# Half of the first V tile loaded by GpSimd's queue instead of SyncE's, at the start of a fused attention and feed-forward kernel

## The chip, the cores and the metric

The kernel runs on one core of a Trainium2 chip. The metric is the device time of one execution in microseconds (us), the median of three runs. Engine names: PE is TensorE (matmuls), PEld its weight load, DVE is VectorE, ACT is ScalarE, POOL is GpSimd, SP is SyncE. "SPq" and "POOLq" are the DMA issues on the queues of SP and POOL.

## What is computed

```python
# q, k, v: 8 batches x 8 heads x 576 tokens x 64, float32
q_c, k_c, v_c = (a.reshape(B, H, nc, 64, D) for a in (q, k, v))      # chunks of 64 tokens
scores = np.matmul(q_c, k_c.transpose(0, 1, 2, 4, 3)) / np.sqrt(D)
attn = exp(scores - max) ; attn = attn / (sum(attn) + 1e-09)
x = np.matmul(attn, v_c)  ->  reshaped to 4608 tokens x 512
h = np.maximum(x @ w_in, 0.0)          # w_in 512 x 2048
out = h * h @ w_out                    # w_out 2048 x 512, result float32
```

Attention never looks across a chunk of 64 tokens, so a block of tokens can go through attention and both matrix products on its own.

## The kernel before

The 4608 tokens are cut into nine blocks of 512 tokens. For each block the kernel computes attention into `xT` (x transposed, bfloat16), then `ffn_in` (x times w_in, 64 matmuls of 128x512 for a block, ReLU on ACT, square on DVE or ACT) and `ffn_out` (times w_out). From the second block on, attention for the next block is woven into the matmuls of the block before it by a table of slots. The order on every engine is the order in which the program calls the operations; no scheduler changes it.

The first block has nothing to hide behind, so it has its own path (lines 656 to 697), in two halves of four heads each, u = 0 and u = 1:

- `load_half` (L227) loads q and k of four heads and 512 tokens with one DMA of 512 KB each, on SP's queue. The calls go q of u=0, k of u=0, q of u=1, k of u=1.
- `load_v_half(u)` (L236) loads V of four heads and 512 tokens into `v_first` with four DMAs of 128 KB, one for each 128 tokens (t = 0 to 3), in rows of 64 float32 (256 bytes). `v_first` is a view of the buffer `w_sum`, which has its real use only later; the profile therefore calls it w_sum. A POOL memset (L220) puts a column of ones beside each head of V.
- `load_w_in(i)` (L162 and the casts at L165) loads 256 columns of w_in (512 KB) on SP's queue into a staging tile `w_st`, of which there are five, and POOL casts it to bfloat16. The first of the eight casts is cut into two pieces, one for each 128 columns. `load_w_out(i)` (L170, cast at L173) does the same for w_out.
- On PE the order is: transposes of q and k of u=0 (L257), scores (L278), transposes of q and k of u=1, `values_half(e0, ..., 0, 0)` (L298: attention weights of u=0 times V, tokens t = 0 and 1), scores of u=1, `values_half(e0, ..., 0, 1)`, transposes of x (L314), `values_half(e1, ..., 1, 0)`, and so on to the last transposes of x at L314. Matmuls on constants (`keep_busy`, L326) stand in between. After them come the 64 matmuls of `ffn_in` (L480). The first two output tiles of `ffn_in` begin with the two quarters of the sum that need only heads 0 to 3.

The DMAs on SP's queue take eight completion counters in turn, so the n-th load carries a wait for the (n-8)-th to have landed. DMAs issued from POOL have counters of their own.

Of the kernel before, what the change touches and what calls it, by code (L numbers as in the profile page):

```python
# [17 lines left out]
def kernel(  # L18
# [9 lines left out]
    nc = tc.nc  # L28
# [130 lines left out]
    def load_w_in(i, n_cast=1):  # L159
        cols = slice(i * 256, (i + 1) * 256)  # L160
        st = wst_pool.tile([128, 1024], FP32, name="w_st").rearrange("p (a f) -> p a f", a=n_dt)
        nc.sync.dma_start(out=st, in_=moe_w_in[:, cols].rearrange("(a p) f -> p a f", p=128))  # L162
        n = 256 // n_cast
        for c in range(0, 256, n):
            nc.gpsimd.tensor_copy(  # L165
                out=w_in_bf[:, :, i * 256 + c:i * 256 + c + n], in_=st[:, :, c:c + n])
# [57 lines left out]
    def load_half(src, u, name):  # L224
        st = in_pool.tile([128, 2, H, D], FP32, name=name)
        b, s = first
        nc.sync.dma_start(  # L227
            out=st.rearrange("p t h d -> p (t h d)").rearrange("p (h e) -> p h e", h=4),
            in_=src[b, 4 * u:4 * u + 4, s:s + BT, :].rearrange("h (s i) d -> s h (i d)", i=4))
        return st.bitcast(BF16).rearrange("p t h d -> p (t h d)").rearrange(  # L230
            "p (h i d) -> p h i d", h=4, i=4)

    def load_v_half(u):
        b, s = first
        for t in range(4):
            nc.sync.dma_start(  # L236
                out=v_first[:, t, 4 * u:4 * u + 4, 0:D],
                in_=v[b, 4 * u:4 * u + 4, s + 128 * t:s + 128 * t + 128, :].rearrange(
                    "h s d -> s h d"))
# [419 lines left out]
    for u in range(2):  # L659
        qh.append(load_half(q, u, "q_sb"))  # L660
        kh.append(load_half(k, u, "k_sb"))
    for u in range(2):
        load_v_half(u)
    load_w_in(0, n_cast=2)
    xTs[0] = att_pool.tile([128, BT // 128, n_dt, 128], BF16, name="xT", bufs=2)
    qkTs = [att_pool.tile([128, 2, 2, n_hp, 128], BF16, name="qkT", bufs=4) for _ in range(2)]
# [146 lines left out]
```

## Time and profile before

| what | value |
|---|---|
| median of 3 runs | 281.04 us (280.75 to 281.83) |
| the profiled execution | 281.17 us, of which its span is 279.4 us |
| PE busy | 269.2 us, 96% of the span |
| DVE, ACT, POOL busy | 186.5, 160.5, 35.8 us |
| DMA moved | 57.09 MB, mean 204 GB/s |
| q1 (the queue that SP issues to) | 83.8% of 16 DMA engines' span |
| q0 (the queue that POOL issues to) | 2.8% of 16 DMA engines' span |
| first matmul of `ffn_in` (L480) | starts 17.63 us into the span |

The span is the time from the first to the last event that the profile shows; 1.8 us of the execution lie outside of it. In answers of the trace, each line names the start, the duration, the engine, the line of the kernel, the operation, its output and input, the number of instructions merged, and in brackets how long the engine was idle before it and what ended that idle time. In the answers by stretch of time, DMA share is the mean busy share of the 16 DMA engines (it can pass 1.00, as packets overlap within an engine).

### The profile page before, as it was taken

How to read it: one execution, taken by the hardware profiler on the slowest of the kernel's cores; microseconds unless marked ns; L12 is line 12 of the kernel's file. 1: busy time of each engine (PE TensorE's matmuls, PEld its weight loads, DVE VectorE, ACT ScalarE, POOL GpSimd, SP SyncE). 2: the span in 40 equal slices, each digit the busy share in tenths (PEclk: the TensorE clock that was granted, in tenths of full speed). 3: DMA queues.
4: the chain of work that ended last, by engine and by line, in shares of the span. 5: the costliest groups of instructions: out<-in, count | busy, mean ns of one | idle time of the engine just before them, and what ended most of it. 6: DMA issues, size and time to landing. Idle time of an engine off the chain costs nothing.

```text
span 279.4 us, 7179 instructions
## 1 busy us (share of the span) xinstructions
PE 269.2 (96%) x2960; PEld 176.2 (63%) x2963; DVE 186.5 (67%) x304; ACT 160.5 (57%) x269; POOL 35.8 (13%) x62
## 2 busy tenths in 40 slices
PE   6789999989999999999999999999999999999994
PEld 4544455878774487448744874487448744874584
DVE  1446414998943595579549954995579649955793
ACT  2537615885348862877197719762877197218710
POOL 2037844240171000000000000000000000000012
PEclk9999999999999999999999999999999999999998
DMA  7999999989999999979999999979699964141003
GB/s 236 220 345 358 364 332 240 326 212 194 255 207 244 238 213 191 258 183 198 218 245 260 187 184 298 191 158 185 196 238 208 212 199 40 39 109 44 0 21 131
DMA packets 144384, 57.09 MB, mean 204 GB/s; under 512 B 110624, under 2 KB 141600, under 8 KB 144352
## 3 DMA queue, kind: packets, MB, share of 16 engines
q1 hardware_dynamic: 143296, 53.62, 83.8%
q0 software_dynamic: 912, 2.88, 2.8%
q8 instruction: 23, 0.38, 0.6%
q10 hardware_dynamic: 144, 0.13, 0.1%
q14 instruction: 9, 0.07, 0.1%
HBM read 36.70 MB, written 9.44 MB: 165 GB/s over the span
## 4 chain that ended last, share of the span: by engine, by line
PE 80%; DVE 6%; SPq 4%; ACT 2%; DMA 2%; issue 2%; POOL 0%; DVEq 0%; ACTq 0%
PE ps_ffn L480 39%; PE ps_ffn L533 32%; PE ps_ffn L626 5%; SPq L236 3%; DMA w_st<-in_moe_w_in_dram 2%; DVE x L409 2%; DVE gT L475 2%; DVE w_st L493 2%; ACT rl L471 2%; PE ps_att L401 2%; PE ps_att L374 1%; ACT e L385 1%; SPq L227 1%; PE ps_att L428 1%; PE ps_att L190 1%
## 5 line engine op out<-in xcount | busy, mean ns | idle before, releaser
L480 PE MATMUL ps_ffn<-xT,w_in_bf 128*128 128x512 bf16 (+1 forms) x640 | 130.0, 358 | 0.7 <-POOL w_in_bf L165 0.7
L475 DVE TENSOR_TENSOR gT<-rl 128x512 bf16<-128x512 f32 (+2 forms) x132 | 74.2, 593 | 61.4 <-ACT rl L471 60.7
L471 ACT ACTIVATE rl<-ps_ffn 128x512 f32<-128x512 f32 (+2 forms) x160 | 85.7, 554 | 26.9 <-PE ps_ffn L480 23.3
L480 PEld LDWEIGHTS <-w_in_bf 128*128 128x128 bf16 x640 | 60.5, 98 | 58.2 <-POOL w_in_bf L165 2.2
L533 PEld LDWEIGHTS <-w_st 128*128 128x128 bf16 x640 | 62.0, 98 | 8.2 <-DVE w_st L493 0.9
L493 DVE TENSOR_TENSOR w_st<-gT 128x2048 bf16<-128x2048 bf16 x40 | 47.3, 1217 | 0.2
L533 PE MATMUL ps_ffn<-w_out_bf,w_st 128*128 128x256 bf16 x384 | 45.1, 273 | 0.1
L533 PE MATMUL ps_ffn<-w_sum,w_st 128*128 128x256 bf16 x256 | 29.6, 273 | 0.0
L616 ACT COPY o_sb<-ps_ffn 128x512 f32<-128x512 f32 (+1 forms) x8 | 4.5, 559 | 40.3 <-PE ps_ffn L533 40.3
L533 PEld LDWEIGHTS <-gT 128*128 128x128 bf16 x256 | 24.8, 98 | 4.4 <-DVE gT L475 0.2
L568 POOL DMA_DIRECT2D out_dram<-o_sb x4 | 2.2, 553 | 186.2 <-DVE o_sb L493 186.2
L409 DVE TENSOR_TENSOR x<-ps_att,rec 128x512 bf16<-128x512 f32 x32 | 22.1, 691 | 1.1
L385 ACT ACTIVATE e<-ps_att 128x1024 bf16<-128x1024 f32 x16 | 15.8, 1022 | 4.8 <-PE ps_att L374 4.8
L473 ACT ACTIVATE gT<-rl 128x512 bf16<-128x512 f32 (+2 forms) x28 | 16.8, 599 | 0.9
L533 PE MATMUL ps_ffn<-w_out_bf,gT 128*128 128x256 bf16 x128 | 15.3, 273 | 0.0
L533 PE MATMUL ps_ffn<-w_sum,gT 128*128 128x256 bf16 x128 | 15.3, 273 | 0.0
L626 PE MATMUL ps_ffn<-w_out_bf,gT 128*128 128x512 bf16 x61 | 14.2, 379 | 0.3 <-issue 0.2
L165 POOL CAST w_in_bf<-w_st 128x1024 bf16<-128x1024 f32 (+1 forms) x9 | 9.0, 1001 | 17.9 <-DMA w_st<-in_moe_w_in_dram 17.9
L340 ACT CAST qkb<-k_sb 128x1024 bf16<-128x1024 f32 x10 | 10.5, 1047 | 1.2 <-DMA k_sb<-in_k_dram 1.2
L333 ACT CAST qkb<-q_sb 128x1024 bf16<-128x1024 f32 x10 | 10.4, 1044 | 0.0
L626 PEld LDWEIGHTS <-gT 128*128 128x128 bf16 x64 | 6.0, 98 | 7.0
L401 PEld LDWEIGHTS <-e 64*64 64x64 bf16 x512 | 5.8, 107 | 6.3 <-DVE x L409 2.1
(63 smaller groups left out, 157.1 us busy)
## 6 DMA issues: line engine op xcount, KB each, us to landing
q_sb<-in_q_dram SPq DMA_DIRECT2D x16, 512.0 KB, 6.2
k_sb<-in_k_dram SPq DMA_DIRECT2D x24, 256.0 KB, 5.8
out_dram<-o_sb SPq DMA_DIRECT2D x20, 256.0 KB, 3.7
w_st<-in_moe_w_in_dram SPq DMA_DIRECT2D x8, 512.0 KB, 6.8
w_st<-in_moe_w_out_dram SPq DMA_DIRECT2D x8, 512.0 KB, 6.1
ve_sb<-in_v_dram SPq DMA_DIRECT2D x28, 128.0 KB, 3.5
vo_sb<-in_v_dram SPq DMA_DIRECT2D x21, 128.0 KB, 3.0
out_dram<-o_sb POOLq DMA_DIRECT2D x9, 256.0 KB, 5.5
```

Source lines behind the costliest of these rows:

```text
L333: copy(out=qkb[:, 0].rearrange("p (i h d) -> p i h d", i=2, h=H), in_=qk[g][0].rearrange("p t h d -> p (t h d)").rearrange("p (h i d) -> p ...
L340: copy(out=state["qkb", g][:, 1], in_=qk[g][1].rearrange("p t h d -> p (t h d)"))
L385: nc.scalar.activation(out=e_out, in_=s_in, func=AF.Exp, scale=scale)
L401: nc.tensor.matmul(out=ps[64 * p:64 * p + 64, a, hp * (D + 1):(hp + 1) * (D + 1)], lhsT=e[64 * c:64 * c + 64, a, hp, t, :], rhs=vb[64 * c: ...
L409: nc.vector.tensor_tensor(out=x[:, t].rearrange("p h a d -> p a h d"), in0=o[:, :, :, 0:D], in1=rec.to_broadcast([128, 2, n_hp, D]), op=AL ...
L471: nc.scalar.activation(out=rl[:, 0:n], in_=h[:, 0:n], func=AF.Relu)
L473: nc.scalar.activation(out=gT[:, ft, c:c + n], in_=rl[:, 0:n], func=AF.Square)
L475: nc.vector.tensor_tensor(out=gT[:, ft, c:c + n], in0=rl[:, 0:n], in1=rl[:, 0:n], op=ALU.mult)
L480: nc.tensor.matmul(out=h[:, 0:n], lhsT=w_in_bf[:, dt, ft * 128:(ft + 1) * 128], rhs=xT[:, c // 128:(c + n) // 128, dt, :], start=(dt == 0) ...
L493: engine.tensor_tensor(out=out, in0=in0, in1=in1, op=op)
L533: nc.tensor.matmul(out=outs[t], lhsT=a[:, i, t * 128:(t + 1) * 128], rhs=b[:, i, :], start=(first and i == 0 and (last or t == 0)), stop=( ...
L626: nc.tensor.matmul(out=o_ps[tt], lhsT=gT[:, ft, tt * 128:(tt + 1) * 128], rhs=w_out_bf[:, ft, :], start=(ft == 0), stop=(ft == n_ft - 1))
```

## The change

V of u=1 (heads 4 to 7) is no longer issued by SP behind the q and k of both halves, but by POOL. In the program its call moves up, to stand after q and k of u=0; on POOL it comes behind the memsets and ahead of the casts of w_in. SP issues q, k, q, k, then the four DMAs of V of u=0, then w_in. In the built program the orders on PE, DVE and ACT are the same as before; SP has four DMAs fewer and POOL four more.

```diff
     def load_v_half(u):
         b, s = first
+        queue = nc.gpsimd if u else nc.sync
         for t in range(4):
-            nc.sync.dma_start(
+            queue.dma_start(
                 out=v_first[:, t, 4 * u:4 * u + 4, 0:D],
...
     for u in range(2):
         qh.append(load_half(q, u, "q_sb"))
         kh.append(load_half(k, u, "k_sb"))
-    for u in range(2):
-        load_v_half(u)
+        if u == 0:
+            load_v_half(1)
+    load_v_half(0)
     load_w_in(0, n_cast=2)
```

## The prediction

> **What bounds the kernel now.** I began with the page. PE is busy for 96% of the span, and the chain of work that ended last is PE for most of its length. What is not PE lies partly at the start: the chain by line names SP's issue of V (L236) and a landing of w_in.
>
> ```profile
> PE 80%; DVE 6%; SPq 4%; ACT 2%; DMA 2%; issue 2%; POOL 0%; DVEq 0%; ACTq 0%
> PE ps_ffn L480 39%; PE ps_ffn L533 32%; PE ps_ffn L626 5%; SPq L236 3%; DMA w_st<-in_moe_w_in_dram 2%; DVE x L409 2%; DVE gT L475 2%; DVE w_st L493 2%; ACT rl L471 2%; PE ps_att L401 2%; PE ps_att L374 1%; ACT e L385 1%; SPq L227 1%; PE ps_att L428 1%; PE ps_att L190 1%
> ```
>
> Second, the chain in order of time for the first 24 us. It runs through SP's eight issues of V, then through the third piece of w_in, its cast, and into PE. After that it holds no load: whatever PE gains or loses before 32 us should reach the end one for one.
>
> ```profile
> 11.86 0.51 SPq L236
> ...
> 13.51 6.92 DMA w_st<-in_moe_w_in_dram
> 20.43 0.05 issue
> 20.49 1.23 POOL w_in_bf L165
> 21.71 0.05 issue
> 21.76 2.33 PE ps_ffn L480 x10
> ```
>
> Third, the timeline of the first 45 us, to see how far behind the other path, attention, is.
>
> ```profile
> 2.11 0.15 POOL L220 MEMSET w_sum<- 128x32 f32 x1
> 2.89 9.48 SPq L236 DMA_DIRECT2D w_sum<-in_v_dram  x8
> 9.85 0.64 PE L257 MATMUL ps_ffn<-ident,k_sb 128*64 128x128 bf16 x16 [0.66 <-DMA k_sb<-in_k_dram]
> 11.03 0.32 PE L298 MATMUL ps_att<-w_sum,e 64*64 64x65 bf16 x8 [0.17 <-DMA w_sum<-in_v_dram]
> 12.41 9.69 SPq L162 DMA_DIRECT2D w_st<-in_moe_w_in_dram  x8
> 16.86 0.40 PE L314 MATMUL ps_ffn<-ident,x 128*128 128x128 bf16 x4 [0.59 <-DVE x L306]
> 17.63 3.85 PE L480 MATMUL ps_ffn<-xT,w_in_bf 128*128 128x512 bf16 x16 [0.38 <-POOL w_in_bf L165]
> 21.76 10.53 PE L480 MATMUL ps_ffn<-xT,w_in_bf 128*128 128x512 bf16 x48 [0.28 <-POOL w_in_bf L165]
> ```
>
> The reader should see two paths that end almost together. Attention waits for q, k and then V (9.85 and 11.03 are moments at which PE was released by a landing) and is through on PE at 16.86 + 0.40 = 17.26. The w_in path releases PE at 17.63.
>
> Fourth, the DMA engines over the same stretch.
>
> ```profile
> 9.00:10.00 1.00, 0.34 (x8) 0.15 (x8) 0.60 (x1) 0.00 (x0) 0.00 (x0) 1.00 1.33 227
> 11.00:12.00 1.00, 0.97 (x42) 0.65 (x41) 0.58 (x2) 0.11 (x1) 0.00 (x0) 1.00 0.81 155
> 12.00:13.00 1.00, 0.68 (x28) 0.58 (x21) 0.44 (x2) 0.89 (x1) 0.00 (x0) 1.00 0.55 125
> 16.00:17.00 1.00, 0.41 (x6) 0.14 (x4) 0.77 (x2) 0.04 (x1) 0.04 (x1) 1.00 1.08 382
> ```
>
> The last two columns are the DMA share and GB/s. The engines are full from 3 us on (share 0.99 to 1.33 in each microsecond from 3 to 11); only while the last of V is issued does the share fall, to 0.81 and 0.55. So there is no free bandwidth beside q and k, and some behind V.
>
> **What the change can give.** It removes four issues from SP: 8.40 to 12.37, 3.97 us, so w_in may be issued at about 8.4 instead of 12.41. The data cannot come that much sooner, since the same bytes are ahead of it; what is recovered is the idle share, (1 - 0.81) + (1 - 0.55) = 0.64 us, and a little at 14 us: w_in some 0.6 to 1.5 us earlier. What that is worth to PE: the start wait, 17.63 - 17.26 = 0.37 us; and the stalls inside the 64 matmuls. Those take 32.29 - 17.63 = 14.66 us, and at the pace of the undisturbed 48 (10.53 / 48 = 0.2194 us) would take 14.04, so 0.62. Together 0.99 us is the ceiling. Behind it the next thing late is attention itself, at 17.26.
>
> **What it costs.** Let d be the delay of attention's end. PE's time to the end of `ffn_in` is then 17.26 + d + 14.04 against 32.29: the change is d - 0.99 us, as long as w_in comes early enough, and with d above 0 it does.
>
> When does V of u=1 start to move? POOL is through with its memset at 2.26. Its stores show the lag from issue to first packet: one issued at 46.05 has none before 48 and the first in 48.0 to 48.3, two issued from 270.97 on have none until 272. So 1.1 to 2.2 us, and V starts at 3.4 to 4.5. In the microsecond from 3 to 4 SP's queue still moves q and k of the first half at 366 GB/s, and k of the second half releases PE only at 9.85. V therefore takes its bandwidth from k of u=0, q and k of u=1, all of which attention needs earlier than V of u=1 (first needed at 13.53).
>
> How much does it take? In the trace of before nothing is loaded by POOL; its stores are the nearest row for sharing.
>
> ```profile
> DMA packets 514, 0.34 MB, mean 340 GB/s; under 512 B 461, under 2 KB 461, under 8 KB 513
> ...
> q0 software_dynamic: 66, 0.21, 57.6%
> q1 hardware_dynamic: 447, 0.11, 51.5%
> ```
>
> This is 49 to 50 us: POOL's queue q0 moves 0.21 MB while q1's loads get 0.11 MB. From 48.2 to 55.2 q0 moves 1.05 MB, 0.15 MB/us, in 40.2% of the engines' time: 1.05 / (7.0 x 0.402) = 0.373 MB/us of engine time. The 53 large packets of the fence (514 less 461) hold nearly all its 0.21 MB, so some 4 KB each, though the rows stored are 1 or 2 KB: this queue joins rows. If V's 0.524 MB move at that price, they cost q1 0.524 / 0.373 = 1.4 us. If they cost what 256-byte rows cost on SP's queue (872 of them in the microsecond from 9 to 10), the 2,048 rows cost 2,048 / 872 = 2.35 us. At 0.15 MB/us V needs 3.5 us, so it is through at 7 to 8, before k of u=1 is: the whole cost falls on k, and V of u=0 stands right behind k as before. I take the middle, d = 1.9, because V has the short rows of the one row and the queue of the other.
>
> [...]
>
> **Edits at nothing.** POOL's four issues cost 0.54 us (128 rows) to 0.71 us (256 rows) each in its stores; by those two rows, 0.17 us for each further 128 rows, 512 rows are 1.05 us, so 4.2 us in all, 2.3 to 6.5. Behind them on POOL stands only the first cast, which waits for w_in until 16.96: covered by over 10 us. The eight counters in turn now make w_in's first load wait for q of u=0 instead of V of u=0; that landed by 4.66, so nothing. All later loads on SP keep their order and come no later than PE.
>
> **The sum.** d - 0.99 = 1.9 - 0.99 = +0.9 us. On the profiled 281.17 this is 282.1; on the median, 0.13 lower, 281.9, which I give. About 0.5% (1.4 us) is what can be told from no change here, so this is "same", on its slow side. By the two ends of d it is +0.4 to +1.4, 281.4 to 282.4.
>
> **Rivals.** First, V slips in unseen: POOL's queue starts late or gets less than it got in 49 to 50, so that k arrives as before. For it: in 51 to 53 q1 kept 0.23 to 0.24 MB/us beside q0; POOL has never loaded short rows here. Against: q0 held 0.15 MB/us over 7 us. Then d is 0 to 1.4 and the time 280.05 to 281.4. Only its extreme end with something added passes 0.5% faster, since the ceiling is 0.99 us.
>
> Second, slower: V of u=0 is delayed on top of k. PE waits for its t = 0 and 1 at 11.03 already now, the one landing of V on which it is idle. If V of u=1 is still moving when k is through, the two queues share: 1,024 rows that need 1,024 / 872 = 1.2 us alone take up to twice that. With the upper price for k, d = 2.35 + 1.2 = 3.55, and the change +2.6, 283.6. It decides from the point where d passes 2.4, 1.4 + 0.99: that is, as soon as the shortfall at `values_half` is more than k's own. For it: the four issues on POOL take until 6.5 by the estimate above, so its last rows could start at 7.6 to 8.7. Against: at 0.15 MB/us V is through earlier.
>
> Third, the change does not do what it says: SP's queue is held up by what is outstanding, not by its count of issues. Its V issues took 0.57, 1.24, 1.43 and 2.10 us where those of q and k took 0.5. With the engines shared, the four that stay could take as long as the eight did, and w_in comes no earlier. With d = 1.9 its waits at PE fall behind attention anyway, unless w_in moves with d too: then +1.9, 282.9.
>
> **How the numbers follow.** The forecast gets 0.58, the first rival 0.17, the second 0.20, the third 0.05. The second and third lie past 1.4 us for nearly all of their chance, the forecast's upper edge for 0.04: slower 0.28. Faster by over 1.4 us needs more than the ceiling: 0.05. The rest, 0.67, is within. The range leaves out the first rival's best end and the top of the second: 280.4 to 283.5.
>
> **What would show it.** Right: q0 packets from 3.4 to 4.5 on; PE released by k of u=1 at 11.3 to 12.2 instead of 9.85; by V of u=0 about 1.2 us behind that; w_in issued before 11; L480 starting at about 19.2 with no wait for POOL, and its 64 matmuls in 14.0 us. Wrong: k at 9.85 still (first rival); V of u=0 more than 2 us behind k (second); w_in issued at 12 or later (third); or the shift at 32 us not reaching the end, which would mean that the chain later on has slack against loads that I do not see.

## The result and the profile after

The changed kernel takes 284.02 us (median of 4 runs, 283.53 to 284.99) against 280.89 us (4 runs beside it): a ratio of 1.011, 95% interval 1.0074 to 1.0147, or +3.1 us. A second set of runs gave 1.010 (1.0066 to 1.0134). The forecast was 281.9 us within 280.4 to 283.5; the measured time lies above that. The profiled execution is the longest of the first four, 284.99 us, with a span of 283.2 us against 279.4. In two of the kernels below (e1_fill, e8_fill_v) two of the twelve executions each were over 1.5% above the fastest, and the ratios leave these out.

The page's chain of work that ended last, by engine:

```profile
PE 65%; DVE 11%; SPq 8%; DMA 8%; ACT 3%; issue 2%; POOL 1%; DVEq 0%; ACTq 0%
```

For its first 53 us it is now a chain of loads, but that is not where the time went: at 47.6 us SP issues the same load of q as before (47.61 against 47.64), while PE begins the second block's `ffn_in` 3.75 us later (53.36 against 49.61). The timeline of the start shows the place. Lines of the kernel are one or two higher than before (L257 is L258, L480 is L481).

```profile
2.58 3.13 POOL L237 DMA_DIRECT2D w_sum<-in_v_dram  x4 [0.30 <-POOL w_sum L220]
8.07 13.38 SPq L162 DMA_DIRECT2D w_st<-in_moe_w_in_dram  x8
8.35 0.39 PE L327 MATMUL ps_ffn<-ident_f,ident 128*128 128x256 bf16 x2
11.02 0.64 PE L258 MATMUL ps_ffn<-ident,k_sb 128*64 128x128 bf16 x16 [2.28 <-DMA k_sb<-in_k_dram]
12.62 0.93 PE L299 MATMUL ps_att<-w_sum,e 64*64 64x65 bf16 x16 [0.96 <-DMA w_sum<-in_v_dram]
15.51 0.43 PE L299 MATMUL ps_att<-w_sum,e 64*64 64x65 bf16 x8 [0.50 <-DMA w_sum<-in_v_dram]
17.02 1.17 POOL L165 CAST w_in_bf<-w_st 128x512 bf16<-128x512 f32 x2 [11.30 <-DMA w_st<-in_moe_w_in_dram]
21.77 0.46 PE L315 MATMUL ps_ffn<-ident,x 128*128 128x128 bf16 x4 [0.28 <-DVE x L307]
22.07 12.25 PE L481 MATMUL ps_ffn<-xT,w_in_bf 128*128 128x512 bf16 x56
```

PE waits 2.28 us for k of the second half, where it waited 0.66 before, then twice for V of heads 0 to 3. It reaches the 64 matmuls of `ffn_in` at 22.07 instead of 17.63. They take 13.98 us (to 36.05; the last line above stops at 34) instead of 14.66, as no wait for w_in is left in them. End of `ffn_in`: 36.05 - 32.29 = +3.76; span: 283.2 - 279.4 = +3.8. So in these two profiles the whole loss is made before 22 us and goes through one for one.

But the waits are only part of it. In the stretches of time, the third column from the right is the granted clock of PE, behind it the DMA share and GB/s:

```profile
9.00:10.00 1.00, 0.00 (x0) 0.00 (x0) 0.15 (x1) 0.00 (x0) 0.00 (x0) 1.00 1.14 260
11.00:12.00 1.00, 0.64 (x16) 0.48 (x16) 0.53 (x1) 0.30 (x1) 0.00 (x0) 0.85 1.27 202
12.00:13.00 1.00, 0.38 (x8) 0.34 (x9) 0.17 (x1) 0.28 (x1) 0.00 (x0) 0.50 1.38 241
15.00:16.00 1.00, 0.50 (x12) 0.42 (x10) 0.03 (x1) 0.74 (x1) 0.00 (x0) 0.50 1.10 340
20.00:22.00 2.00, 1.72 (x24) 1.03 (x23) 0.90 (x2) 0.59 (x1) 1.53 (x2) 0.51 1.10 346
22.00:24.00 2.00, 2.00 (x13) 0.95 (x11) 0.42 (x1) 0.44 (x1) 1.56 (x2) 1.00 1.10 347
```

From 11.7 to 21.9 us PE runs at half its clock; in the profile of the kernel before it was at 1.00 throughout this stage. The same six constant matmuls, before and after:

```profile
14.15 0.82 PE L326 MATMUL ps_ffn<-ident_f,ident 128*128 128x256 bf16 x6
18.24 1.49 PE L327 MATMUL ps_ffn<-ident_f,ident 128*128 128x256 bf16 x6
```

What PE does between k and `ffn_in` is now the path.

DMA of the microsecond from 8 to 9, the second half's q and k against POOL's V:

```profile
DMA packets 219, 0.30 MB, mean 303 GB/s; under 512 B 28, under 2 KB 185, under 8 KB 219
...
q1 hardware_dynamic: 169, 0.16, 60.5%
q0 software_dynamic: 50, 0.14, 45.0%
```

q1 falls to 0.16 MB/us. Before, it moved 0.30 in that microsecond, and 751 of its 858 packets there were already V's short rows; in the microsecond from 7, where both kernels still load q and k, it moved 0.34 before and 0.23 now. In the answers for each microsecond, q0 has no packet before 7 us, then 36, 50, 55, 35 and 16: V moves from 7 to 12.

### The profile page after: what moved, and what is told of

It reads as the page before. It is cut to its first block, busy times and chain, and to the rows that moved or that the text cites. A ratio compares the mean times of both kernels' runs of the same rounds, so it can differ in the third digit from the quotient of the medians.

```text
span 283.2 us, 7186 instructions
## 1 busy us (share of the span) xinstructions
PE 272.1 (96%) x2963; PEld 178.8 (63%) x2963; DVE 188.3 (66%) x304; ACT 160.7 (57%) x269; POOL 41.7 (15%) x66
## 3 DMA queue, kind: packets, MB, share of 16 engines
q0 software_dynamic: 1104, 3.41, 3.6%
## 4 chain that ended last, share of the span: by engine, by line
PE 65%; DVE 11%; SPq 8%; DMA 8%; ACT 3%; issue 2%; POOL 1%; DVEq 0%; ACTq 0%
PE ps_ffn L481 32%; PE ps_ffn L534 30%; DMA w_st<-in_moe_w_in_dram 5%; DVE gT L476 3%; DVE x L410 3%; DVE w_st L494 2%; DMA w_st<-in_moe_w_out_dram 2%; SPq L151 2%; SPq L237 2%; DMA k_sb<-in_k_dram 2%; ACT rl L472 2%; SPq L147 1%; SPq L162 1%; PE ps_att L402 1%; SPq L105 1%
## 5 line engine op out<-in xcount | busy, mean ns | idle before, releaser
L481 PE MATMUL ps_ffn<-xT,w_in_bf 128*128 128x512 bf16 (+1 forms) x640 | 129.6, 358 | 0.0
L481 PEld LDWEIGHTS <-w_in_bf 128*128 128x128 bf16 x640 | 60.8, 98 | 56.8
L494 DVE TENSOR_TENSOR w_st<-gT 128x2048 bf16<-128x2048 bf16 x40 | 48.2, 1240 | 0.2
```

The lines of the kernel that those rows point to most:

```text
L481: nc.tensor.matmul(out=h[:, 0:n], lhsT=w_in_bf[:, dt, ft * 128:(ft + 1) * 128], rhs=xT[:, c // 128:(c + n) // 128, dt, :], start=(dt == 0) ...
L494: engine.tensor_tensor(out=out, in0=in0, in1=in1, op=op)
```

## The experiments

The theories: **A**, k and V come late because V's bytes move beside them, and the idle PE then loses half its clock, both counting; **B**, the late loads alone; **C**, the clock alone.

### The idle time filled (e1_fill)

```diff
     transpose_half(qh[1], qkTs[1][:, 0], [V])
-    keep_busy(2)
+    keep_busy(24)
     transpose_half(kh[1], qkTs[1][:, 1], [V, A], by_token=True)
+    keep_busy(8)
     values_half(e0, xs[0], 0, 0)
```

> The changed kernel with matmuls on constants put into the two places where PE stood idle: 24 instead of 2 behind the transposes of q of heads 4 to 7, and 8 more behind those of k. The loads are as in the changed kernel. Theory A (late data and the halved clock each cost about half): the granted clock stays at 1.00 from 11 to 22 us, PE is still released by k of heads 4 to 7 at about 11.0 and by V of heads 0 to 3, t = 3, at about 15.5, and the first matmul of ffn_in starts at 20.0 to 20.6 instead of 22.07; the time is 1.2 to 2.2 us above the kernel before, about 282.1 to 283.1. Theory B (the loads alone, the clock costs nothing since that stage waits for data and for DVE anyway): it starts at 22 again, 284.0. Theory C (the clock alone): it starts at 18.5 or earlier, 281.0 to 281.5.

Measured: ratio 1.0043 (1.001 to 1.0076) to the kernel before, +1.2 us. Timeline:

```profile
12.14 0.64 PE L258 MATMUL ps_ffn<-ident,k_sb 128*64 128x128 bf16 x16 [0.66 <-DMA k_sb<-in_k_dram]
16.94 0.82 PE L327 MATMUL ps_ffn<-ident_f,ident 128*128 128x256 bf16 x6
19.85 13.98 PE L481 MATMUL ps_ffn<-xT,w_in_bf 128*128 128x512 bf16 x64
```

and stretches:

```profile
12.00:13.00 1.00, 0.86 (x19) 0.74 (x20) 0.40 (x1) 0.17 (x1) 0.00 (x0) 1.00 1.35 222
13.00:14.00 1.00, 1.00 (x23) 0.74 (x21) 0.29 (x1) 0.41 (x1) 0.00 (x0) 1.00 1.19 285
```

k came even later than in the changed kernel, 12.14, yet with the clock at 1.00 `ffn_in` began 2.2 us earlier. B and C fall: by B `ffn_in` would have begun at 22 again, by C at 18.5 or earlier. By the medians the late data alone costs some 1.2 us, and the clock most of the rest of 3.1. This split is rough: the intervals of the two ratios just touch (1.0076 and 1.0074), the second set of the changed kernel begins at 1.0066, and with the two executions that the ratio leaves out (286.18 and 288.41 us, mean clock 0.994) the median of all twelve is 283.14, 1.7 us above the kernel before.

### The changed kernel again (after_again)

> The changed kernel itself once more, on the same chip and beside the same runs of the kernel before as the other three, so that it can be set against them and against the run with the filled idle time. All theories: 1.0 to 1.5% above the kernel before, 2.8 to 4.2 us. Theory A: the granted clock falls to 0.50 between 11 and 13 us for 7 to 10 us; k of heads 4 to 7 releases PE between 10.9 and 12.3.

Measured: 1.010 (1.0066 to 1.0134). PE is released by k at 11.91, the clock is halved from 13.2 to 20.0, `ffn_in` begins at 21.95. From k to `ffn_in` this run takes 10.04 us, the filled one 7.71: 2.3 us, of which 1.02 us are waits for V (0.35, 0.19 and 0.48) that the filled run does not have. In all eleven executions of the changed kernel on record the mean clock over the span is below 0.995 (0.982 to 0.994). The first profile, at 0.982, is the lowest, so its half clock lasted longest.

### PE held idle with the loads as before (e4_hold_idle, e5_hold_fill, e4b_hold_idle, e5b_hold_fill)

These start from the kernel before. A chain of casts on POOL makes PE wait ahead of the second half's k.

```diff
+    held = const_pool.tile([128, 128], BF16, name="held")
+    for _ in range(34):          # 24 in the second pair
+        nc.gpsimd.tensor_copy(out=held, in_=ident_f32)
...
-    keep_busy(2)
+    keep_busy(2)                 # 22 (18 in the second pair) in the filled ones
+    held_ps = ps_ffn.tile([128, 512], FP32, name="ps_ffn")
+    nc.tensor.matmul(out=held_ps[:, 0:64], lhsT=ident, rhs=held[:, 0:64], start=True, stop=True)
```

> The kernel before with its loads untouched, but with PE held idle by construction: behind the transposes of q of heads 4 to 7 and the two constant matmuls, one matmul waits for a chain of 34 small casts on POOL that ends at 10 to 12 us, so that PE stands idle for about 2 us as in the changed kernel. All data has landed when PE goes on. Theory A and C: the clock falls to 0.50 at about 11.7 and comes back some 10 us later; the first matmul of ffn_in starts at 20 to 21 and the time is 1.5 to 2.7 us above the kernel before. Theory B: the clock falls, but the time is within 0.6 us of the kernel before, since the hold of 1.2 us is within the wait for w_in and its stalls (0.99 us).

> As the run with PE held idle, but with 22 constant matmuls instead of 2 ahead of the held one, so that PE is busy for nearly the whole hold. All theories: the clock stays at 1.00, the first matmul of ffn_in starts at 18.2 to 19.2 and the time is -0.2 to +0.8 us against the kernel before, as only the hold itself counts. The difference to the run with PE held idle is the price of the halved clock with the loads as before: 1.3 to 2.2 us by theory A, under 0.3 us by B, 2.5 to 3.3 us by C.

The first pair missed its aim: 34 casts lasted until 14.40, so that PE stood idle for 5.23 us in one and still 3.03 us in the other. Both had the clock halved from 13.4 to 20.2, both began `ffn_in` at 22.93, and the ratios are 1.018 (1.0134 to 1.0226) and 1.0163 (1.0119 to 1.0208). The second pair, with 24 casts:

> The run with PE held idle again, with 24 casts instead of 34: at the 0.355 us that each took the hold should end at 10.6 to 11.2 instead of 14.4, and PE should stand idle for 1.5 to 2.3 us, as in the changed kernel. Loads as in the kernel before. Theory A and C: the clock falls to 0.50 soon after the hold ends and the first matmul of ffn_in starts at 19.5 to 20.8 (hold of 1.0 us, halved clock 1.5 to 2.3 us); time 1.2 to 2.5 us above the kernel before. Theory B: it starts at 18.1 to 18.7 and the time is within 0.6 us of before.

> The same hold of 24 casts, with 18 constant matmuls instead of 2 ahead of it (2.0 us of work), so that PE stands idle for less than 0.5 us. All theories: the clock stays at 1.00, the first matmul of ffn_in starts at 18.1 to 18.7; the time is -0.3 to +0.6 us against the kernel before. The difference to the run with PE idle is the price of the halved clock with loads as before.

Timeline of the idle one (1.66 us idle), then of the filled one:

```profile
10.73 0.19 PE L682 MATMUL ps_ffn<-held,ident 128*128 128x64 bf16 x1 [1.66 <-POOL held L661]
18.50 5.78 PE L480 MATMUL ps_ffn<-xT,w_in_bf 128*128 128x512 bf16 x26
```

```profile
10.73 0.19 PE L682 MATMUL ps_ffn<-held,ident 128*128 128x64 bf16 x1
17.58 3.62 PE L480 MATMUL ps_ffn<-xT,w_in_bf 128*128 128x512 bf16 x16
21.79 2.55 PE L480 MATMUL ps_ffn<-xT,w_in_bf 128*128 128x512 bf16 x11 [0.59 <-POOL w_in_bf L165]
```

Stretches of the idle one:

```profile
12.00:13.00 1.00, 1.00 (x35) 0.54 (x35) 0.90 (x2) 0.11 (x1) 0.00 (x0) 0.50 0.66 137
15.00:16.00 1.00, 1.00 (x25) 0.92 (x25) 0.50 (x2) 0.21 (x1) 0.00 (x0) 1.00 0.99 336
```

With the loads untouched, the clock is halved in this profile after 1.66 us of idle PE, from 11.6 to 15.0, and `ffn_in` begins 0.92 us later than in the filled run. It does not fall every time: the mean clock over the span is 0.991 to 0.994 in seven of the twelve executions of the idle run and 0.997 to 1.000 in the other five and in all twelve of the filled one. The end does not move: 0.9998 (0.9975 to 1.0022) and 1.0007 (0.9984 to 1.0031). Nor does it within the idle run, where the seven have a median of 281.15 us and the five of 281.22. The 0.92 us are swallowed by the wait for w_in, which the filled run still shows (0.59 us at 21.79). Theory A had put 1.2 to 2.5 us on the idle run: a miss. So the fall was not in itself a loss here: it was short, 3.4 us, and slack of about 1 us lay behind it.

### How long the clock stays down (e8_fill_v)

```diff
     transpose_half(kh[1], qkTs[1][:, 1], [V, A], by_token=True)
+    keep_busy(8)
     values_half(e0, xs[0], 0, 0)
     keep_busy(2)
     e1 = scores_half(qkTs[1])
+    keep_busy(6)
     values_half(e0, xs[0], 0, 1)
```

> The changed kernel with constant matmuls only where PE waits for V (8 behind the transposes of k of heads 4 to 7, 6 behind the second scores), and none more in the wait for k itself. Question: why the halved clock lasts 8 to 10 us in the changed kernel and 3.3 us in the run with PE held idle. If it comes back only after some 3 us in which PE is busy all the time (theory A), it still falls at 11.7 to 13 us, since PE stands idle for over 2 us ahead of k, but is back by 16 to 17.5, and the first matmul of ffn_in starts at 20.3 to 21.3: time 1.5 to 2.6 us above the kernel before, less than the changed kernel's 3.1 and more than the 1.2 of the run with all idle time filled. If its length is fixed, it stays at 0.50 until 20 or later and the time is that of the changed kernel or longer.

In the timeline and the stretches:

```profile
11.44 0.64 PE L258 MATMUL ps_ffn<-ident,k_sb 128*64 128x128 bf16 x16 [2.06 <-DMA k_sb<-in_k_dram]
12.01 1.74 PE L327 MATMUL ps_ffn<-ident_f,ident 128*128 128x256 bf16 x8
20.91 3.40 PE L481 MATMUL ps_ffn<-xT,w_in_bf 128*128 128x512 bf16 x15
```

```profile
13.00:14.00 1.00, 1.00 (x16) 0.53 (x16) 0.00 (x0) 0.00 (x0) 0.00 (x0) 0.50 1.06 284
16.00:17.00 1.00, 1.00 (x25) 0.73 (x24) 0.23 (x2) 0.52 (x1) 0.26 (x1) 1.00 1.06 340
```

The clock is down from 12.2 to 15.6 only, about as theory A said, and `ffn_in` begins at 20.91, a microsecond before the changed kernel's. The time did not follow: 1.0103 (1.0069 to 1.0137), no better than the changed kernel. Part of the reason is seen, the eight matmuls put in run at half clock and take 1.74 us on the path, and k came 0.42 us later than in the changed kernel's profile; why the median lies as high as the changed kernel's stays open.

Across the runs the fall has three lengths: 3.4 us (this run, 12.2 to 15.6; 11.6 to 15.0 with PE held), 6.8 (the changed kernel again, 13.2 to 20.0) and 10.2 (its first profile, 11.7 to 21.9). The two longer ones are twice and three times the shortest, so the half clock of the ten profiles in which it fell can be cut into stretches of 3.41 us, a third of the 10.24 us (11.70 to 21.94) of the changed kernel's first profile. In the 3.41 us before the fall PE was busy for 0 (e4_hold_idle) to 2.14 us (e6_swap, below). Stretches after which the clock stayed down have 2.31 to 3.02 us of work, and those at whose end it came back 3.13 us or more. This is a count in ten profiles; what sets these lengths is not shown. In the changed kernel's first profile the waits for V ahead of 12.6 and 15.5 lie in the first two stretches (2.31 and 3.02); here, with these waits filled, PE is busy throughout the first.

### V held back until q has landed (e2_hold_q1)

```diff
-        if u == 0:
-            load_v_half(1)
+    gate = const_pool.tile([128, 64], BF16, name="gate")
+    nc.gpsimd.tensor_copy(out=gate, in_=qh[1][:, 0, 0, 1::2])
+    load_v_half(1)                # on POOL, behind the copy
     load_v_half(0)
```

> The changed kernel, but POOL first copies a few elements of q of heads 4 to 7 and so issues V of heads 4 to 7 only when that q has landed, at about 8 us, when nearly all of q and k is through. Theory A: k of heads 4 to 7 releases PE at 9.6 to 10.1 as in the kernel before, the idle stretch of PE stays under 1.2 us and the clock at 1.00. V of heads 4 to 7 then shares the engines with V of heads 0 to 3 and the first w_in; V of heads 4 to 7 is needed from 13.5 on. The first matmul of ffn_in starts at 17.3 to 18.5; time 280.2 to 281.5. If V of heads 0 to 3 is what counts and not k, it starts at 19 or later with PE waiting for V at 12 to 15, 282 to 283. Theory C: like A.

Measured: 1.0068 (1.0037 to 1.01). k is on time at 9.92 and the clock at 1.00 until 16, but

```profile
15.92 0.32 PE L299 MATMUL ps_att<-w_sum,e 64*64 64x65 bf16 x8 [2.11 <-DMA w_sum<-in_v_dram]
```

PE waits 2.11 us for POOL's V. Issued from 8.77 on, it moved 11 packets in the microsecond from 10, then 31, 5 and 7 (12 to 14 us), while w_in had 0.34 and 0.35 MB/us on q1; only from 14 on did V get 67 and 58. So the forecast missed, but the run shows what makes k late: with V of heads 4 to 7 held back until q is there, k is on time. V then hardly moved beside the w_in that the change lets go first; whether w_in kept it out or POOL's queue was slow by itself is not shown. Behind that wait the clock was halved from 16.2 to 19.6. The first cast of w_in began at 16.43.

### V by ACT's queue (e3_act)

```diff
-        queue = nc.gpsimd if u else nc.sync
+        queue = nc.scalar if u else nc.sync
```

> The changed kernel with V of heads 4 to 7 issued by ACT's hardware queue instead of POOL's. Theory S (the cost belongs to sharing: the bytes of V move beside q and k, whoever issues them): V's 256-byte rows move between 3.5 and 9 us, k of heads 4 to 7 releases PE at 11.2 to 12.6, PE stands idle for over 2 us and the clock halves; 2.5 to 4.5 us above the kernel before. Theory P (the cost belongs to POOL's queue, its late start at 7 us and its packets of 4 KB): k comes at 10 to 10.8, the clock stays at 1.00; 0 to 1 us above the kernel before.

Measured: 1.007 (1.0045 to 1.0095).

```profile
2.30 5.89 ACTq L237 DMA_DIRECT2D w_sum<-in_v_dram  x4
8.22 1.28 ACT L267 ACT_TABLE_LOAD   x1 [8.22 <-DMA q_sb<-in_q_dram]
```

The run does not decide between S and P: the four issues keep ACT until 8.19, its table load and first copy come behind them, and PE waits 2.54 us for that copy (at 10.15) rather than for k. The same loss of clock follows, 11.8 to 18.7.

### Half of V on POOL, without and with filling (e7_half, e9_half_fill)

In these two and the next, `load_v_half` takes the tokens (and here the queue) as arguments, by default all four on SP.

```diff
         if u == 0:
-            load_v_half(1)
+            load_v_half(1, (2, 3), nc.gpsimd)      # t = 2, 3 only
     load_v_half(0)
+    load_v_half(1, (0, 1))                         # on SP
...
-    keep_busy(2)
+    keep_busy(20)                                  # in e9_half_fill only
     transpose_half(kh[1], qkTs[1][:, 1], [V, A], by_token=True)
```

> Half of the change: POOL issues at once only the tokens t = 2, 3 of V of heads 4 to 7 (two DMAs, 256 KB); t = 0, 1 go on SP behind V of heads 0 to 3 and ahead of w_in. If k is late by the bytes of V that move beside it (theory A: 1,024 rows of 256 bytes, 1.2 us of the engines' time), k of heads 4 to 7 releases PE at 10.6 to 11.3 instead of 9.85 (before) and 11.0 to 12.1 (changed kernel), PE stands idle for 1.3 to 2.0 us, the clock may fall for 3 to 5 us; the first matmul of ffn_in starts at 18.2 to 19.8; time +0.3 to +1.5 us against the kernel before. If k is late because a second queue is there at all, whatever its bytes, it comes at 11.5 or later and the time is +2.5 us or more.

```profile
11.06 0.64 PE L257 MATMUL ps_ffn<-ident,k_sb 128*64 128x128 bf16 x16 [2.09 <-DMA k_sb<-in_k_dram]
18.99 5.34 PE L480 MATMUL ps_ffn<-xT,w_in_bf 128*128 128x512 bf16 x24
```

Measured: 1.0023 (0.9991 to 1.0056). k is 1.21 us late for half of V's bytes, against 1.17, 1.59, 2.06 and 2.29 us in the four profiles with all of V by POOL; PE has no wait for V, and the clock is down for 3.4 us.

> The half change (t = 2, 3 of V of heads 4 to 7 by POOL at once, t = 0, 1 on SP) with 20 constant matmuls instead of 2 in the wait for k of heads 4 to 7, so that the clock need not fall. In the profile of the half change w_in's first cast began at 15.94 instead of 16.96, so this version has w_in earlier. Theory A: the clock stays at 1.00, k releases PE at 10.7 to 11.3, the first matmul of ffn_in starts at 18.0 to 18.6 instead of 18.99, the stalls for w_in inside the 64 matmuls are under 0.3 us, and the time is -0.4 to +0.4 us against the kernel before: no gain, since k's delay of about 1.2 us eats the 0.99 us that w_in can give. If it is below -0.5 us it beats both kernels.

Measured: 1.0001 (0.9972 to 1.003). The clock stays at 1.00 from 9 to 16, k comes at 11.41, 1.56 us late and a little outside its forecast, and `ffn_in` at 18.41. No gain is left. With half of V k is thus 1.21 and 1.56 us late, inside the spread with all of it, so these two runs do not show that the delay grows with the bytes. Here w_in's first cast began at 16.77, so its 15.94 in the run before was not to be had twice.

### An earlier w_in alone (e6_swap)

```diff
-    for u in range(2):
-        load_v_half(u)
+    load_v_half(0)
+    load_v_half(1, (0, 1))
     load_w_in(0, n_cast=2)
+    load_v_half(1, (2, 3))
```

> The kernel before with all loads on SP, and only the order on SP changed: the first w_in load (512 KB) goes ahead of the last two DMAs of V (t = 2, 3 of heads 4 to 7, needed by PE from 15.35 us on). It asks what an earlier w_in alone is worth, with no second queue. Theory A: the first cast of w_in starts at 15.2 to 16.2 instead of 16.96, V's last two land at 15 to 16.5, so that PE may wait for V by up to 1 us at the last values; the first matmul of ffn_in starts at 17.2 to 18.0 and the time is -0.5 to +0.6 us against the kernel before. If it comes out below -0.5 us, w_in is worth more than the 0.99 us ceiling lets expect at this place, and this version beats both kernels.

```profile
15.21 1.16 POOL L165 CAST w_in_bf<-w_st 128x512 bf16<-128x512 f32 x2 [12.94 <-DMA w_st<-in_moe_w_in_dram]
18.40 3.62 PE L480 MATMUL ps_ffn<-xT,w_in_bf 128*128 128x512 bf16 x16
22.39 1.90 PE L480 MATMUL ps_ffn<-xT,w_in_bf 128*128 128x512 bf16 x8 [0.38 <-POOL w_in_bf L165]
```

w_in's first piece is 1.75 us earlier and the time the same, 0.9994 (0.9963 to 1.0026). In the profiled run the clock fell here too, from 12.5 to 15.9, and `ffn_in` began at 18.40, later than forecast, though PE's waits (0.46, 0.70 and 0.17 us for q, k and V) are about those of the kernel before (0.47, 0.66, 0.17), which kept the clock in its profile. The fall does not hide a gain: the nine of twelve executions with a mean clock of 0.997 to 1.000 have a median of 281.15 us, and the 24 such of the kernel before beside them 281.20.

The kernel before has a stretch as empty: the emptiest 3.41 us of its first stage (7.70 to 11.11) hold 2.06 us of PE work, no more than the 2.14 us after which this run lost its clock. Why its profile kept the clock is not shown. In 22 of its 95 executions beside the experiments the mean clock is 0.985 to 0.994, and these have a median of 282.1 us against 281.2 for the other 73; where in the span the clock fell in them is not on record. No version tried beats it.

## Why the prediction was wrong, point by point

Set out by the last transposes of x (L314 or L315), which end attention, with the start of `ffn_in` and the span of the profiled run, in us:

| run | last transposes | `ffn_in` starts | half clock lasts | span |
|---|---|---|---|---|
| before | 16.86 | 17.63 | 0 | 279.4 |
| e5b_hold_fill | 17.35 | 17.58 | 0 | 278.9 |
| e6_swap | 18.16 | 18.40 | 3.4 | 279.7 |
| e9_half_fill | 18.18 | 18.41 | 0 | 279.8 |
| e4b_hold_idle | 18.27 | 18.50 | 3.4 | 279.0 |
| e7_half | 18.76 | 18.99 | 3.4 | 280.0 |
| e1_fill | 19.61 | 19.85 | 0 | 281.5 |
| e2_hold_q1 | 20.11 | 20.34 | 3.4 | 282.3 |
| e3_act | 20.56 | 20.80 | 6.8 | 282.0 |
| e8_fill_v | 20.68 | 20.91 | 3.4 | 282.4 |
| after_again | 21.71 | 21.95 | 6.8 | 283.0 |
| changed kernel | 21.77 | 22.07 | 10.2 | 283.2 |
| e4_hold_idle | 22.69 | 22.93 | 6.8 | 285.1 |
| e5_hold_fill | 22.70 | 22.93 | 6.8 | 285.0 |

- **The form of the sum, d - 0.99, was right.** In the changed kernel d = 21.77 - 16.86 = 4.91, so 3.92, and the span grew by 3.8. The table also shows the slack: up to a start of 18.5 the span stays within 0.5 us of the kernel before, from there on it follows to within about 1.2 us. Each row is one execution, and those of one kernel differ by 2 to 4 us (e1_fill: 281.17 to 284.90).
- **The failed step is d, 1.9 us, and what it left out.** It counted bytes alone and took PE's work between k and `ffn_in` as in the trace of before, so that a loss of the clock stood in it at nothing. It came to 4.91, and to 4.85 in the second profile. With the clock kept (e1_fill) d is 2.75, which includes a little of the filling itself; the other 4.91 - 2.75 = 2.16 us are PE at half clock and waits for V that the filling covered. Since k was later in e1_fill, the count from k on is the fairer one: to the last transposes PE needs 7.01 us before, 7.47 in e1_fill, and 10.75 and 9.80 in the two profiles of the changed kernel, in which the waits for V are 1.46 and 1.02. So 2.3 to 3.3 us of d are half clock and V together, and even with the waits for V taken off in full 1.3 to 1.8 us are left to the half clock; the exact share is not shown. No rival had this term. The second rival's 283.6 lies near the measured 284.02 by luck: it added a delay of V to that of k, and V came 1.60 us behind k (12.62 against 11.02; before, 1.18), short of its own sign of more than 2.
- **The delay of k was sized about right:** 1.17 to 2.29 us against 1.4 to 2.35. That V's early start causes it is shown by e2_hold_q1; that it goes by the bytes is not. Where k was least late (1.17), V of heads 0 to 3 was late on top, by the wait of 0.96 us that the second rival described, and again by 0.50 at t = 3.
- **V's start was wrong:** 7 us instead of 3.4 to 4.5. Issued at 2.58, it waited over 4 us; the stores' lag of 1.1 to 2.2 us did not carry over. The rate then was 0.11 to 0.14 MB/us against 0.15, so V was through at 12, not at 7 to 8, and beside V of heads 0 to 3 as well as k. From 8 to 9 q0 took 0.14 of 0.30 MB, under half.
- **w_in:** its issue came at 8.07 (forecast 8.4), but its first cast at 17.02, no earlier than 16.96. Its rows did move earlier, 275 of 1 KB in the microsecond from 13 (350 packets less 75 short ones) against 29 (692 less 663), but the last of the piece landed no earlier: the forecast had taken a gain in throughput for a gain in landing. It cost nothing here, since attention was later, but with w_in landing so the 0.37 us at the start would not have come with d at 0 either.
- **POOL's issues** took 0.75 to 0.90 us each (1.05 forecast) and hid, as said.

## What to carry to other kernels

Work that fills PE's waits is sized to the waits it was built for: before moving loads around such a stage, list PE's waits there and ask what each becomes. Here the wait for k grew from 0.66 to 2.28 us, and the matmuls behind it ran at half clock from 11.7 to 21.9 us; with the wait filled down to 0.66 us (e1_fill) the clock stayed at 1.00. With the DMA engines full (share 1.03), a second queue added no bandwidth here (345 GB/s with two queues in the microsecond from 7, 339 with one), and what it carried early was paid by what was needed first: k of the second half came 1.17 to 2.29 us later. Look for slack too: here about 1 us of delay was free (0.92 us in e4b_hold_idle, at a ratio of 0.9998), and past that point nearly every microsecond reached the end (in the changed kernel's profile +3.76 us at the end of `ffn_in` and +3.8 in the span).

## What was not expected of the hardware

- The half clock came in lengths of 3.4, 6.8 and 10.2 us. The clock fell after PE had been idle for only 1.66 us (e4b_hold_idle), once even with no single wait over 0.70 us after 7 us (e6_swap).
- POOL's queue had no packet for 4.4 us after its issue (2.58 to 7 us) beside an SP queue that kept the DMA engines full (share 0.98 to 1.06 from 3 to 7), and got 5 and 7 packets in two successive microseconds beside w_in in rows of 1 KB (e2_hold_q1, 12 to 14 us), against 50 and 55 beside the end of q and k (the changed kernel, 8 to 10 us).
